# A fixed TensorE order for attention with projections and memory between its steps, mask by matmul, two-bank maxima and exponentials, and one ScalarE table set

## The chip, the core and the metric

The kernel runs on one NeuronCore of a Trainium2 chip. Its engines run side by side, each with an instruction queue of its own: TensorE (PE in the profile; PEld is its weight loading), VectorE (DVE), ScalarE (ACT), GpSimd (POOL) and SyncE (SP), which here issues the DMAs between the chip's memory (DRAM) and the on-chip SBUF. Matmul results land in PSUM, which has eight banks of 512 float32 columns by 128 partitions; DVE, ACT and POOL read and write there or in SBUF. The metric is the device time of one execution in microseconds (us), lower is better.

## What is computed

One transformer block over a sequence of 2048 tokens of 512 channels, with adaptive LayerNorm, a segmented attention with a compressive memory (four segments of 512 tokens, 32 heads of 16), and a bilinear gated FFN of inner size 1376:

```python
mod = (silu(c) @ w_mod)                       # sa, ca, ga, sb, cb, gb: 512 each
h = layernorm(x) * (1 + ca) + sa
# per head, segments s = 0..3, phi(t) = t + 1 if t > 0 else exp(t)
qs, ks, vs = q[s], k[s], v[s]                 # 512 x 16 each
p = softmax(qs @ ks.T * 16 ** -0.5 + mask)    # causal inside the segment
a_mem = (phi(qs) @ M) / (phi(qs) @ z + 1e-6)
o[s] = sigmoid(beta) * a_mem + (1 - sigmoid(beta)) * (p @ vs)
M = M + phi(ks).T @ vs;  z = z + phi(ks).sum(0)
x = x + ga * (o @ wo)
h = layernorm(x) * (1 + cb) + sb
x = x + gb * (((h @ w_gate) * (h @ w_up)) @ w_down)
```

Weights of q and k are drawn large, so that the scores reach far and the softmax needs precise ones.

## The kernel before

**Precision.** Dense products run as three matmuls in the type fp32r (f32r below) over a high and a low half of each operand (hi·hi, lo·hi, hi·lo). For the scores q and k are split into three bf16 planes each; the six pairs of planes that matter are stacked along the contraction: 6 × 16 = 96 partitions. Two more rows (96 and 97) carry minus the row maximum as a high and a low bf16, against rows of ones, so that the product is already the shifted score.

**Stages.** First the modulation vectors, LayerNorm (`ln_norm`, `ln_mod`) and, per segment, v (L498) and q and k by groups of eight heads (L512). ACT, DVE and POOL split q and k into planes (L516 to L519), and one DMA for each writes three planes to DRAM (`kd`, `qd`). The memory M, z and its reading (L534 to L562) follow per group. Then attention, then wo (L337), then the FFN over four segments and 11 tiles of the inner size (L618 gate and up products, L631 the down product).

**Attention** goes by 32 units: segment, group, half a group (four heads).
- `load(u)` (L156 to L165): six DMAs read the planes into one of four buffer pairs `kst`, `qst`; the planes that stand in several pairs are broadcast while loading.
- `qpass(u)` (L167 to L206): the scores with queries on the partitions, for the row maxima. Per head the four diagonal 128 × 128 blocks go to PSUM (`pd`, L171), ACT copies them out (`ds`, L179), POOL masks them (L180), DVE takes the maxima (L192); the blocks below the diagonal are reduced by DVE out of PSUM (L185, L191). The maxima are negated, split, transposed by PE (`ntp`, L200), copied (`nt`, L202), and two small DMAs lay them into rows 96 and 97 of `qst` (L204).
- `kpass(u)` (L236 to L340): transposed scores (keys on the partitions, L249) in one PSUM bank each, ACT's exponential of 128x512 (`pt`, L253), POOL zeroing what the mask forbids (L257), p·v of four heads side by side in PE's four column strips (`tb`, L267), a copy (L302), transposes back (`tr`, L306), the quotient (L308 to L311), the memory's part (L316), and per segment the transposes, splits and wo.

**Order.** The kernel is a set of generators, stepped in a written sequence; within it a scheduler decides the order on each engine from its own model of costs, with priorities (p·v is raised, L267 and above). Two units' maxima lie ahead of the projections' end; in the steady loop `load` stands three units ahead of the k products and `qpass` two ahead. PSUM is three single banks for maxima (`lq`), three for k scores (`lk`), two for everything else (`ms`). All DMAs are issued from SP's queue.

Of the kernel before, what the change touches and what calls it, by code (L numbers as in the profile page):

```python
# [24 lines left out]
NEG = -3.0e38  # L25
SYNC = mybir.DependencyInfo(mybir.DependencyClass.Sync, mybir.DependencyReason.DATA)
ONES2 = 1.0 + 0x3F80 / 2.0 ** 23
# [3 lines left out]
def tile_kernel(ctx, tc, x, wq, wk_, wv, wo, beta, w_gate, w_up, w_down, c, w_mod, out):  # L31
# [10 lines left out]

    cst = ctx.enter_context(tc.tile_pool(name="cst", bufs=1))
# [9 lines left out]
    btag = ("lq", "ms")  # L53

    def bank(name, dt=F32, shape=(P, 512)):
        nbank[0] ^= 1
        return pst(shape, btag[nbank[0]], name, dt)

    ident = cst.tile([P, P], F32, name="ident")
    make_identity(nc, ident)  # L60
    identb = cst.tile([P, P], BF, name="identb")
    nc.vector.tensor_copy(identb, ident)
# [18 lines left out]
    qd = [[dram.tile([3, P, L], BF, name=f"qd{s}_{g}") for g in range(NG)] for s in range(NSEG)]  # L81
    kd = [[dram.tile([3, P, L], BF, name=f"kd{s}_{g}") for g in range(NG)] for s in range(NSEG)]
    memd = [[dram.tile([P, 4 * HG * DH], F32, name=f"memd{s}_{g}") for g in range(NG)] for s in range(NSEG)]
    x1d = [[dram.tile([P, D], F32, name=f"x1d{s}_{t}") for t in range(4)] for s in range(NSEG)]
# [4 lines left out]
    def ln_norm(pool, xt, s, pfx):  # L89
# [7 lines left out]
        nc.scalar.activation(sd, mv[:, :, 1], AF.Sqrt, bias=epst[:, 0:1])  # L97
# [4 lines left out]
        eng = nc.gpsimd if pfx == "a" and s == 0 else nc.vector  # L102
# [4 lines left out]
        eng.tensor_mul(y, y, b)  # L107
        for t in range(4):
# [3 lines left out]
        def transposed():  # L112
            for d in range(KT):
                ps = bank(f"{pfx}tp{s}_{d}")
                for t in range(4):
                    nc.tensor.transpose(ps[:, t * P:(t + 1) * P], xt[t][:, d * P:(d + 1) * P], ident)
                yield ps

        return transposed()

    def ln_mod(pool, hpool, tps, s, sc, sh, pfx, hb):

        hH, hL = [], []
        for d, ps in enumerate(tps):
# [4 lines left out]
            nc.vector.tensor_copy(hi, h)  # L129
            nc.vector.tensor_sub(lo, h, hi.bitcast(F32))  # L130
            hH.append(hi)
            hL.append(lo)
        return hH, hL

    wk = ctx.enter_context(tc.tile_pool(name="wk", bufs=1))
    PT = 12
    vpool, vp = open_pool(name="vp", bufs=1)
    vt = [[vp.tile([P, H * VS + 16], F32, name=f"v{s}_{t}") for t in range(4)] for s in range(NSEG)]
    for s in range(NSEG):
        for t in range(4):  # L140
            nc.gpsimd.memset(vt[s][t][:, 0:H * VS].rearrange("p (h e) -> p h e", e=VS)[:, :, DH], 1.0)
            nc.gpsimd.memset(vt[s][t][:, H * VS:], 0.0)
    MZ = [vp.tile([P, HG, VS], F32, name=f"MZ{g}") for g in range(NG)]
# [3 lines left out]
    stpool, stp = open_pool(name="stp", bufs=1)  # L147
    kst = [stp.tile([98, HQ, L], BF, name=f"kst{i}") for i in range(NB)]
    qst = [stp.tile([98, HQ, L], BF, name=f"qst{i}") for i in range(NB)]
    mxb = [stp.tile([P, HQ, 16], F32, name=f"mxb{i}") for i in range(3)]  # L150
    for a in kst:
        nc.gpsimd.memset(a[96:98].rearrange("p h t -> p (h t)").bitcast(F32), ONES2)
    for a in mxb:
        nc.vector.memset(a, NEG)

    def load(u):  # L156
        s, g, j = u // 8, u // 2 % 4, u % 2
        Q, K = qst[u % NB], kst[u % NB]
        q3 = qd[s][g].rearrange("r (d h) t -> r d (h t)", h=HG)[:, :, j * HQ * L:(j + 1) * HQ * L]
        k3 = kd[s][g].rearrange("r (d h) t -> r d (h t)", h=HG)[:, :, j * HQ * L:(j + 1) * HQ * L]  # L160
        for n, p0 in ((3, 0), (2, 48), (1, 80)):
            nc.sync.dma_start(K[p0:p0 + DH * n].rearrange("p h t -> p (h t)"), k3[0:n])  # L162
        for r0, n, p0 in ((0, 3, 0), (1, 2, 48), (2, 1, 80)):
            nc.sync.dma_start(Q[p0:p0 + DH * n].rearrange("p h t -> p (h t)"),  # L164
                              q3[r0:r0 + 1].to_broadcast([n, DH, HQ * L]))  # L165

    def qpass(u):  # L167
        Q, K, mx = qst[u % NB], kst[u % NB], mxb[u % 3]

        def mm(o, h, qb, k0, n):  # L170
            nc.tensor.matmul(o, Q[0:96, h, qb * P:(qb + 1) * P], K[0:96, h, k0 * P:(k0 + n) * P],  # L171
                             start=True, stop=True)

        for h in range(HQ):
            pd = pst([P, 4, P], "lq", f"pd{u}_{h}", F32)
            for qb in range(4):
                mm(pd[:, qb, :], h, qb, qb, 1)
            ds = stp.tile([P, 4, P], F32, tag="ds", name=f"ds{u}_{h}", bufs=3)
            nc.scalar.activation(ds, pd, AF.Copy)  # L179
            nc.gpsimd.affine_select(ds, ds, pattern=[[0, 4], [-1, P]], compare_op=ALU.is_ge,  # L180
                                    fill=NEG, base=0, channel_multiplier=1)
            p1 = pst([P, 4, P], "lq", f"p1{u}_{h}", F32)
            mm(p1[:, 0, :], h, 2, 1, 1)
            mm(p1[:, 1:4, :].rearrange("p a b -> p (a b)"), h, 3, 0, 3)
            nc.vector.tensor_reduce(mx[:, h, 11:15], p1, axis=AX.X, op=ALU.max)  # L185
            if h % 2 == 0:
                p2 = pst([P, 2, 2, P], "lq", f"p2{u}_{h}", F32)
            mm(p2[:, h % 2, 0, :], h, 1, 0, 1)
            mm(p2[:, h % 2, 1, :], h, 2, 0, 1)
            if h % 2 == 1:  # L190
                nc.vector.tensor_reduce(mx[:, h - 1:h + 1, 7:9], p2, axis=AX.X, op=ALU.max)  # L191
            nc.vector.tensor_reduce(mx[:, h, 0:16:5], ds, axis=AX.X, op=ALU.max)  # L192
            yield
        m = stp.tile([P, 16], F32, tag="m", name=f"m{u}", bufs=2)
        nc.vector.tensor_reduce(m, mx.rearrange("p h (q j) -> p (h q) j", j=4), axis=AX.X, op=ALU.max)
        nb = stp.tile([P, 2, 16], BF, tag="nb", name=f"nb{u}", bufs=2)
        nc.vector.tensor_scalar_mul(nb[:, 0, :], m, -1.0)
        nc.vector.scalar_tensor_tensor(nb[:, 1, :], m, -1.0, nb[:, 0, :], op0=ALU.mult, op1=ALU.subtract)
        tp = pst([32, P], "ms", f"ntp{u}", BF)
        nc.tensor.transpose(tp, nb.rearrange("p a b -> p (a b)"), identb)  # L200
        nt = stp.tile([32, P], BF, tag="nt", name=f"nt{u}", bufs=2)
        nc.vector.tensor_copy(nt, tp)  # L202
        for i in range(2):
            nc.sync.dma_start(Q[96 + i:97 + i].rearrange("p h (q t) -> p (h q) t", t=P),  # L204
                              nt[16 * i:16 * i + 16, :])
        yield  # L206

    NQ = NSEG * NG * 2
    wt = {}

    def prep(i, pool, rpool, tag, nb):
# [3 lines left out]
        for w, nm in ((w_gate, "g"), (w_up, "u")):  # L215
# [6 lines left out]
            r[nm] = (hi, lo)  # L222
        raw = rpool.tile([P, D], F32, tag=tag, name=f"crd{i}", bufs=nb)
# [7 lines left out]
        wt[i] = r  # L231

    oT = {}
    orows, mems = {}, {}

    def kpass(u):  # L236
        s, g, jq = u // 8, u // 2 % 4, u % 2
        ug = u // 2
        h0 = jq * HQ
        Q, K = qst[u % NB], kst[u % NB]  # L240
        if jq == 0:
            orows[ug] = wk.tile([P, 4, HG, DH], F32, tag="orow", name=f"orow{ug}", bufs=2)
            if s > 0:
                mems[ug] = P2["pb"].tile([P, 4, HG, DH], F32, tag="memb", name=f"memb{ug}", bufs=2)
                nc.sync.dma_start(mems[ug].rearrange("p t h e -> p (t h e)"), memd[s][g])
        orow = orows[ug]

        def mm(o, h, kb):
            nc.tensor.matmul(o, K[:, h, kb * P:(kb + 1) * P], Q[:, h, kb * P:], start=True, stop=True)  # L249

        def ex(ps, nm):
            pt = wk.tile([P, 512], F32, tag="pt", name=nm, bufs=PT)
            nc.scalar.activation(pt, ps, AF.Exp, scale=0.25)  # L253
            return pt

# [340 lines left out]
    for _ in steps:  # L596
        pass
# [72 lines left out]
```

## Time and profile before

| what | us |
|---|---|
| three runs | 1086.73, 1092.95, 1093.07 |
| their median | 1092.95 |
| the profiled execution | 1093.67 |
| its span in the profile | 1092.0 |

The mean clock that TensorE was granted in the profiled execution is 0.914 of full speed. In the profile's rows an operation is named by its source line, engine, output and inputs with their shapes; "x320 | 177.8, 623 | 91.9 <-PE k L249 79.6" means 320 instructions, 177.8 us busy, 623 ns for the mean one, 91.9 us during which the engine stood idle just ahead of them, 79.6 of that until a k product of L249 was done. In rows of waits the three numbers are the sum of the idle time in us, the number of waits, and the longest. In the timeline and the chain the first number is the start in us and the second the duration; a matmul's duration is modelled and overlaps the next one, so that their rate is read from start to start. In rows of stretches, each engine's busy time in us stands with its number of instructions, and then the mean granted clock, the share of time in which the DMA engines moved data, and GB/s.

### The profile page before, as it was taken

The page shows a single profiled execution, that of the slowest core. Times are in us where ns is not written, and L with a number is a line of the kernel's source. Part 1 is how long each engine was busy: PE and PEld are TensorE (multiplying, and loading weights), DVE is VectorE, ACT ScalarE, POOL GpSimd, SP SyncE. Part 2 cuts the span into 40 slices and gives each one's busy share as a digit, 9 for nine tenths or more (in the row PEclk, how much of TensorE's full clock was granted, in tenths as well). Part 3 has the DMA queues.
Part 4 walks back from the last instruction along what each step waited for, and adds up shares of the span by engine and source line. Part 5 has one row for each costly group of instructions (what it writes and reads, how often), then busy time and mean ns, then how long its engine had stood idle before and what let it go on. Part 6 is the DMA issues. An engine that isn't in the chain of part 4 may idle for free.

```text
span 1092.0 us, 15409 instructions
## 1 busy us (share of the span) xinstructions
PE 936.4 (86%) x5560; PEld 669.0 (61%) x5560; DVE 558.2 (51%) x1161; ACT 427.3 (39%) x770; POOL 337.8 (31%) x602
## 2 busy tenths in 40 slices
PE   6968999987667867768687868799999999999998
PEld 4757788743333634335343534488878888887886
DVE  9744966784545545645465667336832422332212
ACT  4624453364455445543565556512311211121111
POOL 6521322375344344433454455335510000000000
PEclk9989999976888887879788988999999999999999
DMA  7462622342222231214322341244320002011011
GB/s 261 121 188 81 203 101 87 107 132 74 58 59 53 89 92 53 70 50 112 85 75 65 86 129 52 69 126 122 83 88 28 22 18 77 1 39 39 1 40 39
DMA packets 60797, 89.45 MB, mean 82 GB/s; under 512 B 9168, under 2 KB 33744, under 8 KB 60720
## 3 DMA queue, kind: packets, MB, share of 16 engines
q1 hardware_dynamic: 60576, 88.44, 27.5%
q8 instruction: 44, 0.72, 0.3%
q14 instruction: 33, 0.27, 0.1%
q10 hardware_dynamic: 144, 0.02, 0.0%
HBM read 64.05 MB, written 24.12 MB: 81 GB/s over the span
## 4 chain that ended last, share of the span: by engine, by line
PE 62%; DMA 23%; DVE 6%; SPq 5%; issue 3%; ACT 1%; POOL 0%; DVEq 0%; ACTq 0%; POOLq 0%
DMA qst<-qd 17%; PE gps L618 11%; PE acc L631 11%; PE ups L618 11%; PE k L249 4%; PE tb L267 4%; PE wops L337 3%; PE kps L512 3%; PE p L171 3%; PE qps L512 2%; PE pd L171 2%; PE vps L498 2%; SPq L162 2%; SPq L164 2%; DMA kd<-k 2%
## 5 line engine op out<-in xcount | busy, mean ns | idle before, releaser
L253 ACT ACTIVATE pt<-k 128x512 f32<-128x512 f32 x320 | 177.8, 623 | 91.9 <-PE k L249 79.6
L171 PEld LDWEIGHTS <-qst 96*128 96x128 bf16 x1024 | 82.9, 112 | 150.7 <-issue 109.4
L257 POOL TENSOR_SCALAR_AFFINE_SELECT pt<-pt 128x256 f32<-128x256 f32 (+1 forms) x320 | 114.3, 362 | 122.5 <-ACT pt L253 117.3
L185 DVE TENSOR_REDUCE mxb<-p 128x4 f32<-128x512 f32 x128 | 87.6, 685 | 125.6 <-PE p L171 125.0
L171 PE MATMUL pd<-kst,qst 96*128 96x128 bf16 x512 | 58.5, 244 | 104.0 <-DMA qst<-qd 97.6
L249 PE MATMUL k<-qst,kst 98*128 98x384 bf16 (+3 forms) x512 | 123.7, 339 | 12.7 <-DMA qst<-nt 8.7
L180 POOL TENSOR_SCALAR_AFFINE_SELECT ds<-ds 128x512 f32<-128x512 f32 x128 | 81.8, 641 | 139.3 <-ACT ds L179 136.7
L623 DVE TENSOR_TENSOR gs<-gs,ups 128x512 f32<-128x512 f32 (+1 forms) x44 | 30.2, 687 | 179.7 <-PE ups L618 177.7
L179 ACT ACTIVATE ds<-pd 128x512 f32<-128x512 f32 x128 | 77.6, 612 | 110.4 <-PE pd L171 106.2
L267 PE MATMUL tb<-pt,v 128*32 128x512 f32 (+3 forms) x1024 | 101.2, 500 | 1.0 <-ACT chf L126 0.9
L626 ACT ACTIVATE mH<-gs 128x512 fp32r<-128x512 f32 (+1 forms) x44 | 27.8, 632 | 170.5 <-DVE gs L623 162.5
L192 DVE TENSOR_REDUCE mxb<-ds 128x4 f32<-128x512 f32 x128 | 85.9, 676 | 13.3 <-POOL ds L180 13.0
L171 PE MATMUL p<-kst,qst 96*128 96x128 bf16 (+1 forms) x512 | 85.2, 287 | 2.7 <-ACT ds L179 1.4
L249 PEld LDWEIGHTS <-kst 98*128 98x128 bf16 x512 | 47.8, 108 | 64.0 <-issue 44.3
L618 PE MATMUL ups<-chL,uH 128*128 128x512 f32 (+1 forms) x176 | 69.5, 395 | 4.1 <-DVE chL L130 4.1
L618 PE MATMUL ups<-chH,uH 128*128 128x512 f32 (+1 forms) x176 | 69.4, 394 | 1.0 <-DVE chH L129 1.0
L618 PE MATMUL ups<-chH,uL 128*128 128x512 f32 (+1 forms) x176 | 69.1, 393 | 0.0
L618 PE MATMUL gps<-chH,gH 128*128 128x512 f32 (+1 forms) x176 | 69.1, 393 | 0.0
L631 PE MATMUL acc<-dL,mH 128*128 128x512 f32 (+1 forms) x176 | 69.0, 392 | 0.0
L618 PE MATMUL gps<-chH,gL 128*128 128x512 f32 (+1 forms) x176 | 68.9, 392 | 0.0
L618 PE MATMUL gps<-chL,gH 128*128 128x512 f32 (+1 forms) x176 | 68.9, 392 | 0.0
L631 PE MATMUL acc<-dH,mL 128*128 128x512 f32 (+1 forms) x176 | 68.9, 392 | 0.0
(189 smaller groups left out, 1769.2 us busy)
## 6 DMA issues: line engine op xcount, KB each, us to landing
wm<-in_w_mod_dram SPq DMA_DIRECT2D x24, 256.0 KB
kd<-k SPq DMA_DIRECT2D x16, 384.0 KB
kst<-kd SPq DMA_DIRECT2D x32, 192.0 KB
qd<-q SPq DMA_DIRECT2D x16, 384.0 KB
qst<-qd SPq DMA_DIRECT2D x32, 192.0 KB
x<-in_x_dram SPq DMA_DIRECT2D x16, 256.0 KB
kst<-kd SPq DMA_DIRECT2D x32, 128.0 KB
qst<-qd SPq DMA_DIRECT2D x32, 128.0 KB
```

The lines of the kernel that those rows point to most:

```text
L171: nc.tensor.matmul(o, Q[0:96, h, qb * P:(qb + 1) * P], K[0:96, h, k0 * P:(k0 + n) * P], start=True, stop=True)
L179: nc.scalar.activation(ds, pd, AF.Copy)
L180: nc.gpsimd.affine_select(ds, ds, pattern=[[0, 4], [-1, P]], compare_op=ALU.is_ge, fill=NEG, base=0, channel_multiplier=1)
L185: nc.vector.tensor_reduce(mx[:, h, 11:15], p1, axis=AX.X, op=ALU.max)
L192: nc.vector.tensor_reduce(mx[:, h, 0:16:5], ds, axis=AX.X, op=ALU.max)
L249: nc.tensor.matmul(o, K[:, h, kb * P:(kb + 1) * P], Q[:, h, kb * P:], start=True, stop=True)
L253: nc.scalar.activation(pt, ps, AF.Exp, scale=0.25)
L257: return nc.gpsimd.affine_select(v, v, pattern=[[0, n], [1, P]] if n > 1 else [[1, P]], compare_op=ALU.is_ge, fill=0.0, base=0, channel_mu ...
L267: mm4 = nc.tensor.matmul(tb[32 * j:32 * j + 32, kb * P:], vt[s][kb][:, hh * VS:hh * VS + 32], rhs, start=kb == 0, stop=kb == 3, tile_posit ...
L512: nc.tensor.matmul(ps, a[nm][k][:, gs], b[k], start=n == 0, stop=n == 11)
L618: nc.tensor.matmul(ps[0:n], a[:, k, 0:n], b[k], start=j == 0, stop=j == 11)
L631: nc.tensor.matmul(acc[t], a[0:n, t * P:(t + 1) * P], b[0:n, :], start=i == 0 and j == 0, stop=i == NF - 1 and j == 2)
```

## The change

**PE's order.** Every matmul and transpose outside the FFN goes through `MM` or `TP`, which tie it behind the one before by a dependency without a semaphore, so that PE executes in the order in which the code is written:

```diff
+    def pe(i):
+        if last_pe[0] is not None:
+            tc.add_manual_dep(i.ins, last_pe[0].ins.name, NOSYNC, reason="order")
+        last_pe[0] = i
+        return i
+    def MM(*a, **k):
+        return pe(nc.tensor.matmul(*a, **k))
+    def TP(*a):
+        return pe(nc.tensor.transpose(*a))
```

**The loop.** Attention is cut into small steps, and projections, memory, LayerNorm, wo of segments 0 to 2 and the first FFN weights (`fill_a`, `fill_b`) become generators that yield their estimated PE time; after each of a step's five slots `fill` runs as many as a credit allows, and `until` forces what the next load or transposition needs:

```diff
-    TAGS = {"lq": ("lq", 3), "lk": ("lk", 3), "ms": ("ms", 2)}
+    TAGS = {"lq": ("lq", 1), "lk": ("lk", 1), "tb": ("tb", 1), "ms": ("ms", 2), "sm": ("sm", 1)}
...
+    for v in range(-2, NQ + 1):
+        rate[0] = 10.0 if v < 0 else 5.7
+        if 2 <= v + 3 < NQ:
+            until((v + 3) // 8, (v + 3) // 2 % 4)
+            load(v + 3)
+        on, prev = 0 <= v < NQ, 0 <= v - 1 < NQ
+        for slot in range(5):
+            i = (slot + 3) % 5
+            u = v + 2 if i < 3 else v + 1
+            if 0 <= u < NQ:
+                q_step(u, i)
+            if on:
+                k_step(v, slot)
+            if prev and slot == 0:
+                av_step(v - 1, 1)
+            if prev and slot == 1:
+                av_step(v - 1, 3)
+                av_step(v - 1, 2)
+            if on and slot == 3:
+                av_step(v, 0)
+            if slot == 2 and 0 <= v + 1 < NQ:
+                n_step(v + 1)
...
+            if prev and slot == 4:
...
+                t_step(v - 1)
...
+            fill(1 / SL, slot in (0, 1, 3))
```

`lq` and `lk` are now one tile of two banks each. The loop has 35 values of v: two before the first k product, 32 units, one after.

**Maxima (`q_step`).** Five two-bank tiles per unit instead of ten single ones: scores of two or four heads are written, then the causal mask is added in PSUM by a product of the identity with a 128 × 128 bf16 block of 0 and −3e38, and one DVE reduction reads 128x1024. The copy to `ds` and its select on POOL are gone. `n_step` takes the negated maximum in one instruction, transposes it in float32 and splits it after (two DVE instructions, two DMAs as before).

```diff
+        for b in range(2):
+            MM(qp[:, b, c:c + n * P], identb, cmask if n == 1 else cmask.unsqueeze(1).to_broadcast([P, n, P]),
+               start=False, stop=True, skip_group_check=True)
+        nc.vector.tensor_reduce(o, src, axis=AX.X, op=ALU.max)
```

**Exponentials (`k_step`).** Likewise five of 128x1024 per unit instead of ten of 128x512; the selects on POOL work on strided blocks of the two-bank tile (two, four and one of 256, 256 and 512 columns per unit). `av_step` and `t_step` hold the rest of the old `kpass`.

```diff
+        pt = ap.tile([P, 2, 512], F32, tag="pt", name=f"pt{u}_{i}", bufs=PT)
+        nc.scalar.activation(pt, kp, AF.Exp, scale=0.25)
```

**Planes.** `kd` and `qd` hold all six stacked planes in DRAM (768 KB instead of 384 for each group of a segment), written by three DMAs instead of one; a load is two DMAs instead of six:

```diff
+        for t, d in ((kst[u % NB], kd), (qst[u % NB], qd)):
+            nc.sync.dma_start(t[0:96].rearrange("p h t -> p (h t)"),
+                              d[s][g].rearrange("r (d h) t -> (r d) (h t)", h=HG)[:, j * HQ * L:(j + 1) * HQ * L])
```

The splitting of q and k into planes moves: ACT makes three copies instead of one, POOL two subtractions instead of one, DVE none instead of two (except for the first group).

**The rest.** o goes to DRAM (`od`) per group and is read back for wo, which for segments 0 to 2 runs in the fill and for segment 3 after the loop (`wo_seg`). v has buffers for two segments instead of four. wk and wq are loaded by group. LayerNorm takes the inverse root as exp(−0.5·ln(var + eps)) with the same Newton step, in place of square root and reciprocal; one ScalarE table set is loaded at the start. Outside the first segment, the halves of h are made by ACT and POOL instead of DVE, and the Newton step runs on POOL. The memory's reading uses one PSUM bank (`sm`) in two halves.

```diff
-        nc.scalar.activation(sd, mv[:, :, 1], AF.Sqrt, bias=epst[:, 0:1])
+        nc.scalar.activation(sd, mv[:, :, 1], AF.Ln, bias=epst[:, 0:1])
         y = pool.tile([P, 4], F32, tag="y", name=f"{pfx}y{s}", bufs=2)
-        nc.vector.reciprocal(y, sd)
+        nc.scalar.activation(y, sd, AF.Exp, scale=-0.5)
```

**FFN.** Its products and their number stay and are not tied in order. The four accumulators are halves of the tiles `lq` and `lk`; gate, up and the transposes go round the four banks `ms`, `tb`, `ms`, `sm`. LayerNorm of its first segment and the first two weight tiles are made in the fill.

More of the change, by code (lines that the diff above doesn't have):

```diff
@@ L110, in ln_norm @@
                                     op0=ALU.subtract, op1=ALU.mult)
[L112 to L121, printed above, removed]
+        yield 0.4
         hH, hL = [], []
-        for d, ps in enumerate(tps):
+        for d in range(KT):
+            ps = bank(f"{pfx}tp{s}_{d}")
+            for t in range(4):
+                TP(ps[:, t * P:(t + 1) * P], xt[t][:, d * P:(d + 1) * P], ident)
             h = pool.tile([P, L], F32, tag="hf", name=f"{pfx}hf{s}_{d}", bufs=hb[2])
@@ L167, in qpass @@
[L167 to L206, printed above, removed]
@@ new lines, in until @@
+    def until(*key):
+        while key not in done:
+            credit[0] -= (mem_step() if len(key) == 3 and memq else next(fa)) or 0.0
+    lw = [load_g("k", wk_, 0, nc.vector), load_g("q", wq, 0, nc.vector), load_v()]
+    for w in lw:
+        next(w)
+    more = [load_g(nm, w, g, nc.gpsimd) for g in range(1, NG) for nm, w in (("k", wk_), ("q", wq))]
+    lng = ln(pa, pa, xts.pop(0), 0, ca_c, sa_c, "a", ("h", 8, 2), True)
+    next(lng)
+    next(lng)
+    mod0(0)
+    next(lw[0])
+    next(lng)
```

806 lines of the change are left out of this document (488 added, 318 removed).

## The prediction

> **What bounds the kernel now.** I read the page's head and its chain summary first, then busy time by stretch, then the waits, and then the chain piece by piece.
>
> ```profile
> span 1092.0 us, 15409 instructions
> PE 936.4 (86%) x5560; PEld 669.0 (61%) x5560; DVE 558.2 (51%) x1161; ACT 427.3 (39%) x770; POOL 337.8 (31%) x602
> PEclk9989999976888887879788988999999999999999
> PE 62%; DMA 23%; DVE 6%; SPq 5%; issue 3%; ACT 1%; POOL 0%; DVEq 0%; ACTq 0%; POOLq 0%
> DMA qst<-qd 17%; PE gps L618 11%; PE acc L631 11%; PE ups L618 11%; PE k L249 4%; PE tb L267 4%; PE wops L337 3%; PE kps L512 3%; PE p L171 3%; PE qps L512 2%; PE pd L171 2%; PE vps L498 2%; SPq L162 2%; SPq L164 2%; DMA kd<-k 2%
> ```
>
> PE leads, but a quarter of the chain is DMA, and one load alone (the stacked q and k planes, qst<-qd) holds 17% of it. Where that sits is shown by the stretches: start, projections, attention, FFN.
>
> ```profile
> core 0: us, PE busy (x) PEld busy (x) DVE busy (x) ACT busy (x) POOL busy (x), PEclk, DMA share, GB/s
> 36.30:218.00 181.70, 165.88 (x867) 138.55 (x867) 120.34 (x282) 75.55 (x129) 47.66 (x44) 0.95 0.43 132
> 218.00:708.50 490.50, 365.09 (x2926) 205.91 (x2924) 272.50 (x598) 262.60 (x502) 221.78 (x472) 0.83 0.29 78
> 721.25:1092.00 370.75, 366.16 (x1620) 297.42 (x1619) 128.50 (x212) 71.01 (x114) 42.88 (x30) 1.00 0.17 51
> ```
>
> Projections (91% PE) and FFN (99%) are PE-bound. Attention is not: in 490.5 us PE works 365 at a granted clock of 0.83, and DVE, ACT and POOL are each about half idle. The waits say for what:
>
> ```profile
> PE pd L171 <- DMA qst<-qd: 97.6, 24, 6.3
> PEld L171 <- issue: 109.4, 113, 6.4
> SPq L162 <- PE k L249: 86.4, 14, 11.3
> ```
>
> PE waits 97.6 us for the loads; the queue that issues them waits 86.4 us for k products to give up a buffer. The chain in order of time shows the loop that this makes:
>
> ```profile
> 36.31 2.90 PE kps L512 x12
> ...
> 51.88 9.65 DMA qst<-qd
> 61.60 10.03 DMA kd<-k
> ...
> 420.92 5.03 DMA qst<-nt
> 433.73 7.49 DMA qst<-qd
> 449.23 7.54 DMA qst<-qd
> 460.75 7.82 DMA qst<-qd
> ...
> 519.88 2.31 DMA qst<-nt
> ```
>
> About every 14 us (433.73, 449.23, 460.75) some 7.5 us of a load stand bare: buffer released, load, scores for the maxima, products. So attention runs on a load's latency, and the work that could cover it (projections, memory, wo) was done before or comes after.
>
> **The change part by part.** The new loop takes 33 steps. A full step does the k products of one unit, the maxima of a later one, and the p·v of this and the previous unit, with 1/31 of the projections, memory and wo work between them. PE executes this in the written order, so PE's own work per step is the first term. Rates at full clock:
>
> ```profile
> 1043.77 2.72 PE gps L618 x12
> ```
> ```profile
> 645.11 1.06 PE L267 MATMUL tb<-pt,v 128*32 128x512 f32 x8
> 646.11 0.66 PE L306 MATMUL tr<-ident,tsb 128*128 128x128 f32 x4
> 646.60 0.39 PE L171 MATMUL p<-kst,qst 96*128 96x128 bf16 x4
> 646.82 0.39 PE L171 MATMUL pd<-kst,qst 96*128 96x128 bf16 x4
> ...
> 648.01 0.85 PE L267 MATMUL tb<-pt,v 128*32 128x384 f32 x8
> 648.80 0.60 PE L249 MATMUL k<-qst,kst 98*128 98x512 bf16 x2
> 649.33 0.86 PE L267 MATMUL tb<-pt,v 128*32 128x256 f32 x16
> 650.12 0.83 PE L249 MATMUL k<-qst,kst 98*128 98x384 bf16 x6
> ```
>
> Twelve f32r products of 512 columns take 2.72, so 0.227 each. From start to start: four bf16 products of 128 columns 0.22 (0.055 each), four f32 transposes 0.49 (0.12 each), p·v of four heads 1.00, 0.79 and 0.79. Hence a unit costs:
> - Maxima: per head 1280 columns, for four heads 5120, and the added mask products 16 × 128 = 2048; 56 × 0.055 = 3.1.
> - k products: 5120 columns, 40 × 0.055 = 2.2. p·v: 1.00 + 0.79 + 0.79 = 2.6. Transposes of the result and of the maxima: 0.6.
> - Fill work in the 31 steps: 564 f32r products × 0.227 = 128; 148 transposes × 0.12 = 18; 88 f32 products of 136 columns for the memory, each between a transpose's 0.13 (by columns) and 0.31 (below), taken at the middle 0.23: 20. Together 166, per step 5.35.
>
> Sum 13.8 us a step. The other engines must fit into it:
>
> ```profile
> L185 DVE TENSOR_REDUCE mxb<-p 128x4 f32<-128x512 f32 x128 | 87.6, 685 | 125.6 <-PE p L171 125.0
> L192 DVE TENSOR_REDUCE mxb<-ds 128x4 f32<-128x512 f32 x128 | 85.9, 676 | 13.3 <-POOL ds L180 13.0
> L311 DVE TENSOR_TENSOR orow<-tr,rd 128x256 f32<-128x256 f32 x32 | 13.3, 418 | 0.3
> L253 ACT ACTIVATE pt<-k 128x512 f32<-128x512 f32 x320 | 177.8, 623 | 91.9 <-PE k L249 79.6 <-PE tb L267 10.6 <-POOL ds L180 0.7
> L97 ACT ACTIVATE csd<-cmv,epst 128x4 f32<-128x4 f32 x4 | 1.2, 298 | 0.4 <-DVE cmv L95 0.4
> L97 ACT ACT_TABLE_LOAD x5 | 6.4, 1283 | 0.1
> L180 POOL TENSOR_SCALAR_AFFINE_SELECT ds<-ds 128x512 f32<-128x512 f32 x128 | 81.8, 641 | 139.3 <-ACT ds L179 136.7
> L257 POOL TENSOR_SCALAR_AFFINE_SELECT pt<-pt 128x256 f32<-128x256 f32 x192 | 78.0, 409 | 86.9 <-ACT pt L253 82.5
> L519 POOL TENSOR_TENSOR k<-kr,k 128x512 bf16<-128x512 f32 x16 | 20.4, 1278 | 67.4 <-DVE k L518 49.6 <-ACT gab L445 8.5 <-DVE mt L562 5.2
> L534 PE MATMUL up<-MZ,phq 128*128 128x136 f32 x96 | 15.3, 309 | 1.0 <-DVE phq L526 0.6 <-DVE nb L198 0.4
> ```
>
> - **Maxima over two banks.** No 1024-column reduction exists here. From below: 256 columns cost 0.418 and 512 cost 0.685, 0.267 more, so 1024 cost 0.685 + 2 × 0.267 = 1.22. From above: twice 0.685, 1.37. I take 1.22, since the slope is of the same engine reading the same kind of memory. Five replace ten: 6.1 for 6.8, with a copy (ACT) and a select (POOL, 0.64) per head gone.
> - **Exponentials over two banks.** 4 columns cost 0.298, 512 cost 0.623; the slope gives 0.95 for 1024, doubling gives 1.25. I take 1.0; five are 5.0 for 6.2.
> - **DVE in all.** Its busy time from 36.3 to 708.5 is 120.3 + 272.5 = 392.8; less the three maxima groups (87.6, 85.9 and half as many at the same price, 43) 176 stay, 5.5 per unit at most, since the change hands part of it (splitting q, k and h) to ACT and POOL. 6.1 + 5.5 = 11.6 of 13.8. ACT: 338.2 in the same stretches less 177.8 is 160 or 5.0 per unit, with 5.0 of exponentials 10.0; four copies to ds (2.5) go and the three moved conversions per projection come in. POOL: the selects fall by 4 × 0.64 = 2.6 per unit, one more subtraction per projection (1.28) comes in; it was at 269 in 672. None of the three reaches PE's sum, so I cost them at nothing beyond stalls; the cover is 2 us on DVE, and without it rival B holds.
> - **One bank pair each for maxima and k products** (three single banks before): the next scores must wait for the reduction of the last. A slot is a fifth of a step, 2.8 us; scores 0.6, pipeline 0.3, reduction 1.22 need 2.1. For the exponential 0.45 + 0.3 + 1.0 = 1.75. Both fit unless another instruction of 0.7 to 1.4 is ahead of them. Behind a late one everything on PE queues, as the order is fixed. Between zero and the whole cover lost (B), I take the PE share of the stretch where PE already ran among such neighbours: 165.88 of 181.70, 0.913. Then a step is 13.8 / 0.913 = 15.1. That row's clock of 0.95 is inside this number.
> - **Loads.** Two instructions instead of six, issued at the head of step v for unit v + 3, while buffers of v − 1 come free at its end; scores of that unit start 1.4 steps, 21 us, later. The bare 7.5 to 10 us of a load vanish behind that. If they didn't, 7.5 a step would return. What is late next is PE itself.
> - **The row of maxima (nt)**: a DMA of 2.31 to 5.03 us, after which k products may start. It is issued in slot 2 for the next step, about 2.9 slots or 8.7 us ahead; 2 us for reduction, transpose and two copies and 5.03 at worst make 7. Covered by 1.7 us, and behind it the whole PE order waits: rival C.
> - **Planes to DRAM**: three writes for each of 32 projections, 768 KB instead of 384. They lie on the same SP queue as loads and rows; one write of before took 10.03. They have a step or more of lead in the fill order. Attention used 78 GB/s where the projections used 132, so volume alone is no bound.
> - **o through DRAM**, double v buffers, LN by logarithm and exponential: off PE, hidden by the same fill lead. Table loads are 1.28 us each; five at this line were 6.4 us of ACT, which had idle time, so nothing.
> - **FFN**: its products aren't chained and keep their kind and number; 370.75 stays. Its cover is PE's own 366.16.
>
> Start: projections begin at 36.31. Until the first scores: 24 products (5.4), the split (about 3), writing and loading the planes, between 2 × 2.31 as the cheapest transfer here and 10.03 + 9.65 as two exposed ones; 49 to 64. The 48 v products (10.9) run meanwhile, to 53. I take 54. The two lead steps hold 54 f32r products (12.3), maxima of 1.6 units (5), and memory (3): step 0 at 74, bounds 62 and 85. The Trainium skill, "DMA: Bandwidth & Descriptors", on why a DMA increments its semaphore by 16, says a transfer spreads over as many of 16 engines as divide its outermost dimensions; by it the old pieces with 3 and 2 rows outermost ran on few engines and the new 96-row loads run on all. No row here shows engines one by one; by an estimate from it the load would fall from 9.65 to under 4 and the sum by 6.
>
> End: the last step and wo of segment 3: 60 products (13.6), 20 transposes (2.4), k products and p·v (4.8), five exponentials and the quotient's chain bare (some 10): 31.
>
> Sum: 74 + 31 × 15.1 (468) + 31 + 371 = 944, and the profiled run's 1093.67 lies 1.7 above its span: **945**. That run is 0.7 above the median, so no correction. Own bounds: steps without stalls (13.8) from 62 give 895; 16.4 from 74 give 985.
>
> **Rivals.**
> - **A, the clock stays at attention's 0.83.** For: gaps around single bank pairs, each product group waiting for a reader. Against: 0.83 was granted at 74% busy PE, 0.95 at 91%. 13.8 / 0.83 + 1.3 of stalls = 17.9; 74 + 555 + 37 + 371 + 2 = 1039. The Trainium skill, "TensorE: Matmul & The Clock Gate", on its second failure mode (cycling of PSUM queues), says a PE that idles briefly between groups while it goes round banks lets the clock swing; the trace's dip in attention agrees in kind, at 0.83. Chance 0.13.
> - **B, the vector engine is the bound.** Reduction at 1.37, slots serial: 5 × (0.6 + 0.3 + 1.37) = 11.4, and 5.5 of other DVE work never beside it: 16.9 a step; 74 + 524 + 31 + 371 + 2 = 1002. For: 125.0 us of idle DVE before L185 show that each reduction follows PE closely. Against: other work can run while PE writes scores. 0.14.
> - **C, slower: the maxima row queues behind the transfers.** One SP queue carries loads, plane writes and nt. If nt waits for a write (10.03) and then takes 5.03, 2 + 10.03 + 5.03 = 17.1 against 8.7: 8.4 us of PE standing in every step, which absorbs the other stalls; 13.8 + 8.4 = 22.2; 74 + 688 + 31 + 371 + 2 = 1166. It decides from 19.9 a step ((1092 − 74 − 31 − 371) / 31). Against: writes come 1 per step or fewer, at 2.31 the row was alone. 0.07, with 0.04 for a step near 20, no change.
>
> **How the numbers follow.** Forecast 0.62. The range starts at 895 and goes over B to half of A, 1020, which leaves out about 0.19. Runs of before span 1086.73 to 1093.07, 0.6%, so 1% either way is about what can be told from no change: faster 0.62 + 0.13 + 0.14 = 0.89, same 0.04, slower 0.07.
>
> **What would show it.** Right: the loop over about 470 us with PE at 90%, clock 0.95 or more, loads of planes gone from the chain, two-bank reductions near 1.22 and exponentials near 1.0. A: PE's digits at 8 or 9 with a clock of 0.83. B: waits of PE on the maxima's DVE reduction of 3 us or more a step, DVE over 85%. C: k products waiting on qst<-nt in nearly every step. Wrong altogether: FFN other than 371, or step 0 past 90.

## The result, and the profile after

| | before | after |
|---|---|---|
| median of the runs, us | 1092.07 (4 runs, 1086.73 to 1093.07) | 1003.45 (4 runs, 1000.53 to 1009.88) |
| ratio to before | 1 | 0.9206 (95% interval 0.9151 to 0.926) |
| span of the profiled execution, us | 1092.0 | 1001.1 |

The changed kernel is 8% faster; 945 was forecast, with 895 to 1020 as the range. Page of the changed kernel: span, busy time, clock in 40 slices, and the chain of waits by engine and by line.

```profile
span 1001.1 us, 14320 instructions
PE 931.2 (93%) x5527; PEld 649.0 (65%) x5528; DVE 493.2 (49%) x841; ACT 393.4 (39%) x563; POOL 287.8 (29%) x429
PEclk8899999798998999999899999999999999999999
PE 76%; DMA 8%; DVE 7%; ACT 3%; issue 3%; POOL 3%; SPq 1%; DVEq 0%; POOLq 0%; ACTq 0%
PE ups L831 12%; PE gps L831 12%; PE q L59 8%; PE tb L59 6%; PE k L59 5%; PE vps L59 4%; PE qps L59 3%; PE wops L59 3%; PE kps L59 3%; DMA wm<-in_w_mod_dram 3%; DVE mxb L230 2%; PE acc3lq L844 2%; PE acc1lk L844 2%; PE acc1lq L844 2%; PE acc0lk L844 2%
```

The load of the planes, 17% of the chain before, is no longer among its lines; PE's share rises from 62% to 76%. The first k product starts at 77.6, and the fixed loop takes 519.5 us for 31 steps, counted from the first k product of one unit to that of the next. The main body of the FFN starts at 629.4. Stretches of the changed kernel, columns as in the prediction: the whole loop, the long steps 6 and 8, four ordinary ones (18 to 21), the long steps 23 and 29, and the FFN.

```profile
core 0: us, PE busy (x) PEld busy (x) DVE busy (x) ACT busy (x) POOL busy (x), PEclk, DMA share, GB/s
77.60:597.10 519.50, 471.34 (x3436) 285.01 (x3433) 316.94 (x544) 279.73 (x379) 211.63 (x330) 0.96 0.45 139
170.80:194.70 23.90, 19.39 (x120) 11.52 (x118) 14.84 (x33) 9.74 (x15) 8.97 (x17) 0.79 0.42 134
212.50:233.50 21.00, 16.64 (x123) 10.65 (x121) 13.84 (x23) 11.63 (x17) 9.00 (x12) 0.86 0.64 194
382.60:443.50 60.90, 59.70 (x442) 35.92 (x442) 35.70 (x62) 31.72 (x41) 23.26 (x38) 1.00 0.40 122
459.30:485.10 25.80, 15.72 (x105) 8.79 (x104) 11.38 (x21) 11.87 (x17) 13.43 (x17) 0.84 0.69 223
561.40:583.60 22.20, 16.65 (x128) 10.55 (x126) 10.09 (x16) 13.07 (x18) 9.34 (x13) 0.92 0.13 37
629.40:1001.10 371.70, 365.50 (x1609) 295.26 (x1607) 120.82 (x192) 68.28 (x113) 41.35 (x42) 1.00 0.16 51
```

In the four ordinary steps (15.2 us each) PE is busy 59.7 of 60.9 us at full clock: there the other engines wait for PE. In the long ones it is idle and slowed down. All 31 steps, in us, from the starts in the timeline:

```
15.8 17.6 14.6 14.9 16.4 13.9 23.9 17.8 21.0 16.1 14.6 15.8 14.6 15.3 23.6 16.9
16.9 15.4 15.3 14.6 14.8 16.1 15.9 25.8 16.5 15.2 15.2 15.5 13.8 22.2 13.5
```

24 of them lie at or below 17 us, mean 15.3. Seven lie above, mean 21.7, and hold 45 us more than seven ordinary ones. Steps are numbered from 0 here. What PE stood for in the loop (total us, times, longest):

```profile
PE mz L59 <- DVE mem L631: 9.0, 5, 3.5
PE q L59 <- DVE mxb L230: 8.2, 11, 2.8
PE tr L62 <- DVE mem L631: 6.5, 3, 4.4
PE op L62 <- DMA orl<-od: 5.2, 3, 4.7
PE up L59 <- DVE phq L587: 4.4, 2, 3.2
```

Only the second row belongs to attention's own chain. The others are instructions of the fill, or transposes that share a bank with it. Step 6, PE and then DVE, from the timeline (start, duration):

```profile
177.46 0.39 PE L59 MATMUL qps<-ahL,wqH 128*128 128x512 f32 x1
181.31 2.15 PE L59 MATMUL mz<-v,pkr 128*128 128x136 f32 x8 [3.46 <-DVE mem L631]
183.26 1.06 PE L59 MATMUL q<-kst,qst 96*128 96x512 bf16 x2
```
```profile
178.00 0.55 DVE L134 TENSOR_SCALAR x<-x,amv,ay 128x512 f32<-128x512 f32 x1 [0.34 <-POOL ay L131]
178.54 2.29 DVE L134 TENSOR_SCALAR x<-x,amv,ay 128x512 f32<-128x512 f32 x3
180.75 0.41 DVE L631 TENSOR_TENSOR mem<-up,den 128x256 f32<-128x256 f32 x1
```

The memory's update mz wants the one bank `sm`, which still holds the memory's reading up. Its reader on DVE (mem) stands behind four LayerNorm instructions of the next segment, which the scheduler has put into DVE's queue two steps before PE needs them. PE's order is fixed, so the scores, k products and projections behind mz stand too. Step 14 repeats step 6 with the next segment (a wait of 3.5 us), and step 8 is the same with a transpose tr behind a modulation sum that waits for its weights (4.4 us). In step 23 PE waits 3.2 us for the memory's query `phq` and then 4.7 us for o from DRAM; in step 29 transposes of o and of the FFN's first LayerNorm wait for ACT and DVE, 2.5 us at most.

### The profile page after: what moved, and what is told of

Read it like the earlier page. It is cut to its first block, busy times and chain, and to the rows that moved or that the text cites. A ratio compares the mean times of both kernels' runs of the same rounds, so it can differ in the third digit from the quotient of the medians.

```text
span 1001.1 us, 14320 instructions
## 1 busy us (share of the span) xinstructions
PE 931.2 (93%) x5527; PEld 649.0 (65%) x5528; DVE 493.2 (49%) x841; ACT 393.4 (39%) x563; POOL 287.8 (29%) x429
## 4 chain that ended last, share of the span: by engine, by line
PE 76%; DMA 8%; DVE 7%; ACT 3%; issue 3%; POOL 3%; SPq 1%; DVEq 0%; POOLq 0%; ACTq 0%
PE ups L831 12%; PE gps L831 12%; PE q L59 8%; PE tb L59 6%; PE k L59 5%; PE vps L59 4%; PE qps L59 3%; PE wops L59 3%; PE kps L59 3%; DMA wm<-in_w_mod_dram 3%; DVE mxb L230 2%; PE acc3lq L844 2%; PE acc1lk L844 2%; PE acc1lq L844 2%; PE acc0lk L844 2%
## 5 line engine op out<-in xcount | busy, mean ns | idle before, releaser
L230 DVE TENSOR_REDUCE mxb<-q 128x8 f32<-128x1024 f32 x160 | 195.6, 1222 | 140.3 <-PE q L59 138.8
L264 ACT ACTIVATE pt<-k 128x1024 f32<-128x1024 f32 x160 | 163.5, 1022 | 189.7 <-PE k L59 189.5
L59 PE MATMUL q<-kst,qst 96*128 96x128 bf16 (+2 forms) x640 | 100.1, 280 | 12.9 <-DVE mxb L230 12.2
L59 PE MATMUL k<-qst,kst 98*128 98x384 bf16 (+3 forms) x512 | 99.3, 307 | 1.8 <-ACT pt L264 1.8
L59 PEld LDWEIGHTS <-qst 96*128 96x128 bf16 x640 | 46.6, 100 | 54.0 <-issue 50.6
L835 ACT ACTIVATE gs<-gps 128x512 f32<-128x512 f32 (+1 forms) x44 | 26.2, 598 | 110.2 <-PE gps L831 110.2
L59 PE MATMUL q<-cmask,identb 128*128 128x128 bf16 (+1 forms) x320 | 55.9, 256 | 0.0
L59 PEld LDWEIGHTS tb<-pt,v 128*32 128x32 f32 x1024 | 22.5, 110 | 35.8 <-issue 28.4
L840 DVE TENSOR_TENSOR mL<-gs,mH 128x512 fp32r<-128x512 f32 (+1 forms) x44 | 31.4, 714 | 26.7 <-ACT mH L839 26.6
L59 PEld LDWEIGHTS <-identb 128*128 128x128 bf16 x320 | 30.8, 100 | 17.7 <-issue 1.1
```

The source lines that it names most:

```text
L59: return pe(nc.tensor.matmul(*a, **k))
L230: nc.vector.tensor_reduce(o, src, axis=AX.X, op=ALU.max)
L264: nc.scalar.activation(pt, kp, AF.Exp, scale=0.25)
L835: nc.scalar.activation(gs[0:n], pss[0][0:n], AF.Copy)
L840: nc.vector.tensor_sub(mL[0:n], gs[0:n], mH[0:n].bitcast(F32))
```

## The experiments

Theory 1 is that reading: a few late fill instructions, each holding up all of PE. Theory 2 is that the excess is spread over all steps by the single bank pairs and the clock. Times are medians of four executions; ratios are to the kernel before, run in the same batch (medians 1098.54 in the first, 1098.11 in the second and 1101.32 in the third). In the third batch the changed kernel ran again.

> The changed kernel once more, beside the three others of this call: 0.92 of the kernel before.

Measured 1004.29 us, 0.9112 (0.9073 to 0.915). It agrees with 1003.45 in microseconds; its ratio is lower since the kernel before was slower in that batch. Microseconds are therefore compared with these two, and ratios where the distance is small.

**pin: DVE's early work tied to its place.**

```diff
-            nc.vector.tensor_scalar(xt[t], xt[t], ...)
+            nrm = nc.vector.tensor_scalar(xt[t], xt[t], ...)
+            if not fast:
+                pin(nrm)
...
-        nc.vector.tensor_scalar_mul(a, r[0], s_c[:, 0:1])
+        pin(nc.vector.tensor_scalar_mul(a, r[0], s_c[:, 0:1]))
```

> The four normalizing DVE instructions of LayerNorm (segments 1 to 3 and the FFN's first) and the modulation sums are tied behind the PE instruction ahead of them, so that DVE executes them where they are written and not two or three steps early; LayerNorm then gets one slot without fill before its transposes. Theory 1 (the excess over 15.1 us a step sits in some long steps, in which the fixed PE order stands behind an instruction that waits for the one PSUM bank sm, whose DVE reader is queued behind early LayerNorm or modulation work): steps 6, 8 and 14 fall from 21 to 24 us to 15 to 17, the time falls by 15 to 25 us against the changed kernel, to 978 to 988. Theory 2 (the excess is spread over all steps, by single bank pairs and the clock, and a wait removed uncovers the next): within 5 us of 1003.

Measured 1010.05 us, 0.92 (0.9129 to 0.927): no gain, some 6 us more. Steps 6, 8 and 14 did fall, from 23.9, 21.0 and 23.6 to 18.3, 18.2 and 17.6. But steps 3 and 11 rose from 14.9 and 15.8 to 23.8 and 22.8: the modulation sums, tied directly ahead of their use, now made PE wait. Step 16 rose too, from 16.9 to 20.6. The rows of its waits:

```profile
PE sbc L59 <- DVE wm L460: 3.9, 1, 3.9
PE mz L59 <- DVE mem L635: 3.4, 5, 1.0
PE gbps L59 <- DVE wm L460: 2.4, 1, 2.4
```

The wait of mz for mem fell from 9.0 to 3.4 and that of tr from 6.5 to 2.1, so the cause of steps 6, 8 and 14 is shown; the edit paid for it elsewhere. Both theories had missed the second half.

**upact: ScalarE empties the bank.**

```diff
+                ups_ = pa.tile([P, 2, HG, VS], F32, tag="upc", ...)
+                nc.scalar.activation(ups_, up, AF.Copy)
+                up = ups_
```

> ScalarE copies each memory product up out of the bank sm at once, and DVE works on the copy. Theory 1 by its other end: the bank comes free whatever DVE has queued, so the PE waits for it in steps 6, 7, 8, 14, 15 and 16 go (about 15 us of waits and the slow clock behind them): 980 to 990. ACT gains 24 copies of about 0.45 us, which it has idle time for. Theory 2: within 5 us of 1003, since mz and tr would wait for something else.

Measured 996.21 us, 0.9061 (0.9004 to 0.9118): some 8 us gained, half of what theory 1 gave. The waits for mem are gone from the list; part of them came back as waits of the next scores for the reduction (12.2 us in the whole changed kernel, 17.9 here), which now stands behind the same DVE work:

```profile
PE q L59 <- DVE mxb L230: 17.9, 16, 2.8
PE up L59 <- DVE orow L314: 3.6, 1, 3.6
```

So the bank was one way by which DVE's early work reached PE, and the maxima are another.

**gap: o is loaded three slots earlier, and a second buffer for h.**

```diff
         yield from prep(0, bc, pb, "cr", 2)
+        for _ in range(3):
+            yield None
         yield from w[0]
...
-("h{}", 1, 1)
+("h{}", 1, 2 if s == 0 else 1)
```

> Three slots without fill between the loads of o for wo of segment 0 and their first transposes, and two buffers instead of one for the scaled h of the FFN's first LayerNorm. Theory 1 (operands of fixed-order fill work that arrive just in time cost their whole lateness): step 23 loses its 5 us wait for the load of o and step 29 its 4 to 5 us of waits for ACT and POOL; 990 to 996. Theory 2: within 3 us of 1003.

Measured 1003.65 us, 0.9129 (0.9065 to 0.9193): not told from the changed kernel by the median; the profiled execution took 998.45. Step 23 fell from 25.8 to 16.2 and step 29 from 22.2 to 16.8, as expected; steps 24 to 26 rose by 8 us together (20.8, 17.0, 17.4). In step 24 PE waits 3.6 us for the split of o on DVE, which stands behind conversions of FFN weights that wait for their loads.

**all: the three together.**

> The three edits together. Theory 1: the gains of pin and upact overlap (both free sm), that of gap adds: 968 to 978, mean step of at most 15.7 us. Theory 2: above 990.

Measured 1004.02 us, 0.9129 (0.9066 to 0.9192): missed. Steps 3, 11 and 16 (24.1, 23.0, 21.5) and 24, 25 (22.7, 19.5) carry what pin and gap had moved there, and step 8 is at 20.8 again, with 3.0 us of waiting for the maxima. Moving an instruction is not enough; it needs room on both sides.

**spread: each load and chain gets room.** All DVE work of the fill that waits for a load is tied at least a slot behind it, and spread (the edit shortened):

```diff
+                        r = load_mod(2 * s)
...
+                        for w in gv:
+                            yield w
+                            n += 1
+                            if n == 8:
+                                yield from mod_acc_fill(r)
+                        a_mod_use(s - 1, 0, r[0])
...
+                pin(nrm)
+                yield 0.6
...
-        rate[0] = 10.0 if v < 0 else 5.7
+        rate[0] = 10.0 if v < 0 else 6.8
```

> All edits that theory 1 asks for, with room: ACT empties up; LayerNorm's statistics and normalization, the modulation sums and the first FFN weights' conversions are tied to places at least a slot behind the loads or chains they need and spread over slots; the loads of o lead their transposes by three slots; the fill rate is raised from 5.7 to 6.8 so that as much stays for after the loop as before. Theory 1: no step above 19 us, mean step 15.3 to 15.8, time 965 to 985. Theory 2: not below 995.

Measured 983.88 us, 0.8954 (0.8922 to 0.8987): at the upper end of the time. The steps missed: their mean is 16.3, and steps 9 and 14 (19.9 and 20.2) stayed above 19. One very long step was left, step 24 with 27.7 us, in which PE waits for o again. Its row of waits, and from the chain (start, duration) a load of wo's weights, which are issued just ahead of those of o:

```profile
PE op L62 <- DMA orl<-od: 6.3, 4, 5.7
```
```profile
459.42 7.22 DMA wor<-in_wo_dram
```

That load of 256 KB takes 7.22 us; some 3 MB (wo, o, two FFN weights and the next planes) are on their way together. That their number is the reason is argued; it was not tried, since in the next run, too, they go out together.

**spread2: more slots between the loads of o and their use.** The loads of the FFN weights were to move behind them, too.

```diff
-        yield next(p)
-        yield None
-        yield None
-        yield None
+        for _ in range(5):
+            yield None
         yield from mixed(p, w[0], 3)
```

> As spread, but the first FFN weights are loaded five slots after the loads of wo and o instead of together with them, since step 24 of spread stood 6 us for o behind 3 MB of other loads. Theory 1: step 24 falls from 27.7 to 18 to 21 us, 6 to 9 us less than spread, 0.887 to 0.891 of the kernel before. Otherwise (the wait returns elsewhere) 0.895.

Measured 976.66 us, 0.8864 (0.8834 to 0.8894), the fastest of all kernels here: 27 us less than the changed kernel. Step 24 took 17.6. But the loads did not move apart: only their place in the code did. From the timelines of spread, then of spread2, the issue of the first FFN weight and the first transposes of o:

```profile
464.11 0.38 SPq L341 DMA_DIRECT2D crg<-in_w_gate_dram  x1
468.21 0.48 PE L62 MATMUL op<-ident,orl 128*128 128x128 f32 x1 [5.67 <-DMA orl<-od]
```
```profile
464.75 0.38 SPq L341 DMA_DIRECT2D crg<-in_w_gate_dram  x1
470.50 1.37 PE L62 MATMUL op<-ident,orl 128*128 128x128 f32 x8
```

The first load of o takes 7.6 us from issue to landing in spread (460.6 to 468.2) and 7.2 in spread2 (461.4 to 468.6). What changed is the transposes' place: PE came to them at 462.5 in spread and stood, and at 470.5 in spread2, when o had landed. So the lead mended step 24, and not lighter traffic. The steps above 17 us hold 26 us more than as many ordinary ones, for 45. The stretch of its 31 steps, by columns as before:

```profile
73.20:567.90 494.70, 455.82 (x3416) 277.76 (x3416) 315.21 (x552) 288.56 (x406) 215.11 (x337) 0.98 0.47 145
```

Of the 25 us that the loop is shorter, PE's idle time makes 9 (48.2 to 38.9). The clock, 0.98 for 0.96, makes another 10 or so.

**noorder and spread2n: the ties between PE instructions left out**, in the changed kernel and in spread2.

```diff
     def pe(i):
-        if last_pe[0] is not None:
-            tc.add_manual_dep(i.ins, last_pe[0].ins.name, NOSYNC, reason="order")
-        last_pe[0] = i
         return i
```

> Only the ties between PE instructions are left out, the loop and everything else stay; the scheduler decides PE's order from its own model. If the written order carries the gain, much of it goes back: 1040 or more, with PE waiting for a load or a reader in many steps. If the loop's sequence, the two-bank tiles and the mask product carry it, within 15 us of the changed kernel; the long steps of theory 1 would then shrink, since a late fill instruction no longer holds up the others.

> spread2 without the ties between PE instructions; the ties of the DVE work to places in the sequence stay. If ties only hurt where a fill instruction is late, little is left to gain: within 6 us of spread2. If the scheduler's order is better in itself, as leaving the ties out of the changed kernel suggests (0.907 for 0.921), 10 us less or more than that. If it was better there only since it steps around late instructions, it is now slower, as it bunches the fill.

noorder took 997.25 us, 0.9068 (0.9045 to 0.9092): 6 to 7 us less than the changed kernel. spread2n took 989.46, 0.8982 (0.8949 to 0.9015): 13 us more than spread2. Two stretches of noorder show what the scheduler does, two steps with no fill at all and one with 79 projection products:

```profile
127.80:149.80 22.00, 18.08 (x169) 9.60 (x167) 15.14 (x22) 11.21 (x12) 5.96 (x14) 1.00 0.30 84
357.30:385.90 28.60, 28.60 (x177) 20.54 (x176) 10.15 (x19) 16.91 (x26) 13.62 (x17) 1.00 0.42 126
```

It bunches the fill. A step without any takes 11.0, of which PE works 9.0: the slot's chain through reduction and exponential, bare. With late fill instructions about, the scheduler's order is 6 to 7 us better, since it can step around them; once they are on time, the written order is 13 us better.

**planes3: three planes in DRAM and six loads, as before the change.**

```diff
-            for r0, n, k in ((0, 3, 0), (3, 2, 0), (5, 1, 0)) if nm == "k" else ...:
-                ...
+            nc.sync.dma_start(dst[s][g].rearrange("r p t -> p r t"), q3)
```

> Only the planes as before the change: three planes of each projection in DRAM by one write of 384 KB, six loads that broadcast them. The prediction held loads and plane writes to be hidden behind 1.4 steps of lead: within 6 us of the changed kernel, loads of 7 to 10 us in the trace but not on the chain. Rival: the two-instruction loads are what took the load off the chain; then up to 7.5 us a step come back, 1050 or more.

Measured 1032.08 us, 0.9395 (0.9378 to 0.9411): 28 us more than the changed kernel, between the two. In the loop the load itself is hidden as forecast, but other things became late. At the start it is not: the first load stands on the chain with 7.93 us, and step 0 comes at 83.4 instead of 77.6, which is 6 of the 28 us. Two of its waits, and the load of modulation weights on its chain; then the same load on the chain of the changed kernel:

```profile
PE mz L59 <- DVE mem L630: 12.8, 5, 4.7
PE q L59 <- DMA qst<-qd: 2.2, 1, 2.2
```
```profile
99.52 8.36 DMA wm<-in_w_mod_dram
```
```profile
91.66 5.91 DMA wm<-in_w_mod_dram
```

PE waits 2.2 us for planes in the whole run, but this load takes 8.36 us for 5.91, and PE's waits for DVE grow (those of mz for mem from 9.0 to 12.8). What does that, the number of the loads, how they spread, or the one write in place of three, was not tried.

**onebank: each two-bank reduction and exponential as two of one bank.**

```diff
-        nc.scalar.activation(pt, kp, AF.Exp, scale=0.25)
+        for b in range(2):
+            nc.scalar.activation(pt[:, b], kp[:, b], AF.Exp, scale=0.25)
```

> Each two-bank reduction and exponential is done as two of one bank (128x512), in the same two-bank tiles. By the prediction DVE and ACT had room (6.1 becomes 6.8 and 5.1 becomes 6.2 us a unit), so 0 to 10 us more than the changed kernel. Rival B (the vector chain sets the slot): the reduction's part of the chain grows by 0.15 us a slot, the exponential's by 0.2, so 25 to 30 us more.

Measured 1009.2 us, 0.9183 (0.9145 to 0.9222): 5 us more in microseconds, not told from the changed kernel by the ratio (0.9206 and 0.9112), and inside the first expectation either way. The vector chain is not what sets a step. Groups of the changed kernel, then the same work in onebank:

```profile
L230 DVE TENSOR_REDUCE mxb<-q 128x8 f32<-128x1024 f32 x160 | 195.6, 1222 | 140.3 <-PE q L59 138.8
L264 ACT ACTIVATE pt<-k 128x1024 f32<-128x1024 f32 x160 | 163.5, 1022 | 189.7 <-PE k L59 189.5
```
```profile
L270 ACT ACTIVATE pt<-k 128x512 f32<-128x512 f32 x320 | 173.4, 594 | 187.4 <-PE k L59 187.1
L232 DVE TENSOR_REDUCE mxb<-q 128x4 f32<-128x512 f32 x256 | 164.8, 684 | 100.2 <-PE q L59 99.0
```

**nomask: the mask products left out.**

```diff
-        for b in range(2):
-            MM(qp[:, b, c:c + n * P], identb, cmask ..., start=False, stop=True, ...)
```

> The mask products are left out, so the maxima are taken over keys behind the query too and the output is not the reference's; nothing else changes. By the prediction PE's own work sets an ordinary step, and the 10 mask products cost 0.97 us of it: 25 to 30 us less than the changed kernel. Rival: ordinary steps are set by waits between the engines (scores, reduction, next scores), and PE's saved time becomes waiting: less than 10 us.

Measured 985.83 us, 0.8955 (0.8917 to 0.8992): 18 us less, between the two. The 0.97 was too high: in the timeline of step 18 the mask products take 0.87 from start to start. In steps in which PE never stands (2, 10, 12 and 19) the whole of it is seen, 14.6 becomes 13.7 or 13.8. So such a step is PE's own work, as forecast. In the loop PE is busy 25.5 us less, and the loop is 20.4 us shorter:

```profile
77.90:577.00 499.10, 445.83 (x3134) 265.06 (x3131) 319.50 (x544) 278.93 (x377) 210.54 (x329) 0.96 0.47 144
```

The other 5 us became idle time of PE (53.3 for 48.2); it grew most in steps 9 (0.8 to 3.4) and 15 (1.7 to 3.3).

## Why the prediction was right, point by point

- **Direction and bound: right.** The planes' load left the chain, PE became the bound (59.7 of 60.9 us in the four ordinary steps), and none of rivals A, B or C came. The clock is 0.96 in the loop, not 0.83, and 1.00 in those steps (against A); five reductions and five exponentials more for each unit cost 5 us and not 25 (against B); no row of k products waiting for the maxima row stands among PE's waits in the loop (against C).
- **The time is rival B's, by chance.** B gave 1002. But B's signs are missing: DVE is busy 61% of the loop (316.94 of 519.5) and not over 85%, and PE waits 8.2 us for the maxima's reduction in all 31 steps and not 3 in each.
- **Start, end, FFN: right.** Step 0 at 77.6 (forecast 74), 32.3 from the last step to the FFN's main body (31), FFN 371.7 (371). Together 6 us of the 58 by which 1003 lies above 945.
- **Prices of the two-bank instructions: right.** 1.222 for 1.22, 1.022 for 1.0. That they matter little, also: two banks in one instruction are worth 5 us together, or nothing that the ratio tells.
- **The term that was mis-sized: the steps, 31 × 15.1 = 468, measured 519.5.** The forecast was 13.8 us of PE work and 1.3 of stalls. Measured in the loop: 48.2 us without PE work and some 20 us lost to the clock of 0.96, together 69, where 31 × 1.3 = 40 were allowed; the rest, 450, is 14.5 us of work at full clock a step. So some 29 of the 51 us are stalls and 22 are PE's work.
- **The stalls** failed where the allowance was taken from a stretch of the kernel before ("the PE share of the stretch where PE already ran among such neighbours: 165.88 of 181.70, 0.913"). It has no place for a step that stands for a load or a DVE queue, and seven of those lie 45 us above ordinary ones. The prediction named the condition, "Behind a late one everything on PE queues, as the order is fixed", and then priced it by the mean of a kernel in which the order was not fixed. That the 24 other steps take 15.3, close to 15.1, is luck: PE is idle in them for only 0.65 us on average, and works 14.7.
- **PE's work**, forecast at 13.8, was priced too low. A projection product among bf16 work costs more than 0.227. Rows of step 13 (starts):

```profile
299.79 0.50 PE L59 MATMUL kps<-ahH,wkH 128*128 128x512 f32 x1
300.12 0.39 PE L59 MATMUL kps<-ahH,wkL 128*128 128x512 f32 x1
300.35 0.40 PE L59 MATMUL kps<-ahL,wkH 128*128 128x512 f32 x1
300.59 0.61 PE L59 MATMUL q<-kst,qst 96*128 96x512 bf16 x2
```

  The first of a group takes 0.33 to the next start, the others 0.23 and 0.24. That is 0.02 to 0.04 us more a product in pieces of six and three, some 0.5 a step. In step 18 the k products take 2.46 us for 2.2, the transposes 0.4 for 0.6, and p·v 2.56 for 2.6. The fill isn't even, either: the 24 ordinary steps hold 19.5 projection products on average, the seven long ones 14.
- **O through DRAM and LayerNorm, "off PE, hidden by the same fill lead": wrong.** LayerNorm's DVE work reached PE in steps 6 and 14, the load of o in step 23, both kinds in step 29; a modulation sum did in step 8. Giving all of them room, with ACT emptying the bank, brought 27 us (spread2).
- **"If they didn't, 7.5 a step would return": the loads are hidden in the loop, but not free.** With the old planes and loads PE waits 2.2 us for planes, and yet 28 us were lost. The lower price of a load, under 4 us, estimated from a rule of the Trainium skill ("DMA: Bandwidth & Descriptors", on why a DMA increments its semaphore by 16), was not reached: the median from issue to landing of the q planes' load is 5.1 us. In the direction the runs agree with it, since the first load of planes3 takes 7.93.

What carries the 89 us was not isolated by one run. The written order does not (noorder is faster), nor do two banks in one instruction (5 us); the new planes with their loads are worth 28. That the rest is the projections and memory standing between the attention steps is argued from noorder's rows, where a step without fill leaves PE idle for 2 of 11 us and a step with fill for none; it was not tried by itself. The old path of the maxima (copy by ACT, select by POOL) was not put back either, so what the mask by matmul is worth stays open.

## What to carry to other kernels

A fixed order on one engine turns every late input of that engine into time for all that is behind it. So the work that feeds it on other engines needs a fixed place as well, with room between a load, the work on it and its use; tying an instruction right ahead of its use only moved the wait here. When pricing such an order, look for its latest input in each step, and not for a mean share of stalls from a kernel that could step around them. Judge a moved wait by the whole list of steps: pin and gap mended the steps that they aimed at and gained nothing, and the three edits together gained nothing, until the places that they moved to were mended too. And look in the timeline whether an edit moved what it was to move: spread2's loads were issued where they had been.

## What the runs showed of the hardware

A longer stall of PE can be paid twice. Three stretches of step 6 of the changed kernel: the wait for mz, what follows, and the rest.

```profile
177.50:181.30 3.80, 0.35 (x2) 0.02 (x1) 3.46 (x8) 2.88 (x5) 1.73 (x4) 0.78 0.32 109
181.30:189.70 8.40, 8.14 (x35) 4.43 (x35) 3.68 (x6) 2.05 (x2) 3.36 (x6) 0.50 0.34 111
189.70:194.70 5.00, 5.00 (x35) 3.79 (x32) 1.99 (x4) 1.43 (x2) 0.76 (x2) 0.98 0.16 51
```

After 3.46 us without work the clock granted is 0.50 for 8.4 us of nearly full work, and then 0.98 again: 4.2 us lost beside the 3.5 of the wait. The Trainium skill, "TensorE: Matmul & The Clock Gate", on how the clock's oscillation bites in real kernels, gives about 3.4 us of idle time as the point from which the clock drops to half. The trace agrees for this stall, but a shorter one did it too. Two stretches of step 29, a wait of 2.50 us and 3.4 us shortly behind it:

```profile
568.70:571.20 2.50, 0.01 (x1) 0.01 (x1) 0.00 (x0) 1.09 (x3) 1.26 (x1) 1.00 0.00 0
572.20:575.60 3.40, 3.04 (x16) 2.14 (x14) 2.29 (x4) 2.67 (x5) 1.85 (x2) 0.50 0.01 2
```

In gap, on the other hand, 3.2 us without work (462.1 to 465.3) left the clock at 1.00. So no single length of the wait decides it here. The second failure mode that the Trainium skill names there (short idle times while cycling through PSUM banks), which the prediction set beside rival A, isn't seen: the four ordinary steps, with one bank pair for the scores, have a clock of 1.00.
